# A recurrent attention and a routed mixture of experts on one core: rows gathered by a table of slots, two experts begun during the routing, experts in order of count

## The chip, the cores and the metric

The kernel runs on one core of a Trainium2 chip. The metric is the device time of one execution in microseconds (us). The execution whose profile is shown below took 533.19 us; three other runs took 536.93, 541.19 and 535.67 us.

## The reference

Four sequences of 768 tokens with 8 heads of 48 go through a recurrence with a gate for each channel. Its output, 3072 rows of 384, is the input of a mixture of 16 experts (4 groups of 4). Each token goes to one expert: the best group, and in it the best expert.

```python
f = 1.0 / (1.0 + np.exp(-f_logit))
for t in range(S):                                   # S = 768
    state = f[:, :, t, :, None] * state + np.einsum('bhd,bhe->bhde', k[:, :, t], v[:, :, t])
    y[:, :, t] = np.einsum('bhd,bhde->bhe', q[:, :, t], state)
x = y.transpose(0, 2, 1, 3).reshape(B * S, H * D)    # 3072 x 384
g_idx = np.argmax(x @ w_group, axis=1)               # 4 groups
e_idx = np.argmax(xg @ w_expert[g], axis=1)          # 4 experts in the group
h = np.maximum(xg[mask_e] @ w1[g, e], 0.0)           # 384 -> 1024
out[tok_idx] = (g_w * e_w)[:, None] * (h @ w2[g, e]) # 1024 -> 384
```

Everything is float32. With the inputs of the case the 16 experts get 166 to 243 tokens each.

## The kernel before, in words

**Attention.** The 768 steps are cut into 6 chunks of 128, and each chunk into two units of two sequences, so 12 units. A unit goes through six stages, each written as a Python generator: `gated` (L285 loads f, k, q, v; L289 to L291 the logarithm of the gate; L297 `cs`, its running sum by a matmul with a triangle; L306 and L308 scale q and k into `qh` and `kh`), `turned` (L319 transposes), `scored` (L339 scores `ap`, masked at L341), `weighed` (L355 and L360 the output `y`, L370 the new state), `done` (L391 transposes back, L398 and L403 the router's logits), `routed` (the function `route`). In iteration i of the loop unit i is in `gated`, unit i-1 in `turned`, and so on. The list `WEAVE` says in which order the stages of one iteration take their steps. From that the framework makes one instruction list for each engine; an engine works through its list in order, and so does the queue SP, which issues nearly all the DMAs.

**Routing.** `route` finds, by two one-hot masks, the expert of each token, and by matmuls with a strict triangle (L163 and L166, `rk`) its place among the tokens of that expert; `run` carries the counts from chunk to chunk. L188 then scatters the rows (384 values, the token's number and its weight) to that place in `xs_dram`, a table in DRAM with room for all tokens at every expert. There are four such indirect DMAs for each chunk, issued by POOL. Because an expert's block may be only partly filled, `clear` (L203 and L204) writes zeros over its first 200 rows beforehand, 32 DMAs issued from SP in iterations 2 to 5.

**Experts.** After the loop `fetch` (L556) reads each expert's first 200 rows from `xs_dram`, and the 16 passes follow each other in a fixed order, then two spare passes of 128 rows (`K2 = 2`) for what is beyond 200. A pass is `turn_in` (L581 transposes the rows), `up` (L592, 24 matmuls of width 200, with Relu), `down` (L604, 24 of them), `turn_out` (L611 transposes back, L613 scales, L614 scatters to the output). The weights of three passes are held at a time. `beyond` (L213 to L249) works out what is beyond 200; a loop after it handles what is beyond the spare passes, and does not run with these inputs.

Of the kernel before, what the change touches and what calls it, by code (L numbers as in the profile page):

```python
# [10 lines left out]
FP32 = mybir.dt.float32  # L11
# [11 lines left out]
def kernel(  # L23
# [26 lines left out]
    W = 200  # L50
    K2 = 2
    NOV = K2 + NT + GE - 1
# [5 lines left out]
    assert D == 48 and S % P == 0 and DM == H * D and DM % P == 0 and N == B * S and G == 4 and EG == 4  # L58
# [4 lines left out]
    wp = ctx.enter_context(tc.tile_pool(name="wp", bufs=2))  # L63


    xs_dram = dp.tile([GE * N + P, RW], FP32, name="xs_dram")
# [13 lines left out]
    strict = const([P, P], FP32, "strict")  # L80
# [5 lines left out]
    make_upper_triangular(nc, strict, val=1.0, diag=False)  # L86
    make_identity(nc, ident)
    nc.vector.tensor_copy(strictb, strict)
# [30 lines left out]
    first = iota([P, 4], [[-1, 4]], "first", base=4)  # L119
    firsts = const([P, B * (G + 1), 4], FP32, "firsts")  # L120
    nc.gpsimd.tensor_copy(firsts, first.unsqueeze(1).broadcast_to((P, B * (G + 1), 4)))
    base = iota([P, GE], [[N, GE]], "base")
    lane = iota([P, 1], [[0, 1]], "lane", mult=1)
# [5 lines left out]
    run = const([P, GE], FP32, "run")  # L129

# [3 lines left out]
    def route(c, bs, lgs, rows, sb):  # L134


        nb = len(bs)
        lg, rows = lgs[:, bs[0]:bs[0] + nb, :], rows[:, bs[0]:bs[0] + nb, :]

        def tmp(shape, name, dtype=FP32):  # L140
            return sb.tile(shape, dtype, tag=f"{name}{nb}", bufs=1, name=name)

        SHP = (P, nb * (G + 1), 4)
        L = lg.rearrange("p n (a e) -> p (n a) e", e=4)
        mx = tmp([P, nb * (G + 1)], "mx")
# [4 lines left out]
        nc.vector.scalar_tensor_tensor(out=oh, in0=dl, scalar=0.0, in1=firsts[:, 0:nb * (G + 1), :], op0=OP.is_ge, op1=OP.mult)  # L150
        nc.scalar.activation(dl, dl, AF.Exp)
        yield
        best = tmp([P, nb * (G + 1)], "best")
        nc.vector.reduce_max(out=best, in_=oh, axis=AX)
        nc.vector.tensor_tensor(oh, oh, best.unsqueeze(2).broadcast_to(SHP), OP.is_equal)
        ohv = oh.rearrange("p (n a) e -> p n a e", n=nb)
        ohe = tmp([P, nb, GE], "ohe", BF16)
        nc.vector.tensor_tensor(ohe.rearrange("p n (g e) -> p n g e", e=EG), ohv[:, :, 1:G + 1, :],
                                ohv[:, :, 0, :].unsqueeze(3).broadcast_to((P, nb, G, EG)), OP.mult)
        yield  # L160

        rk = bank([P, nb + 1, GE], "rk")
        nc.tensor.matmul(rk[:, 0:nb, :].rearrange("p n e -> p (n e)"), lhsT=strictb, rhs=ohe.rearrange("p n e -> p (n e)"), start=True, stop=False, skip_group_check=True)  # L163
        for n in range(nb):
            for m in range(n + 1, nb + 1):
                nc.tensor.matmul(rk[:, m, :], lhsT=onesb, rhs=ohe[:, n, :], start=False, stop=(n == nb - 1), skip_group_check=True)  # L166
        pick = tmp([P, nb, GE], "pick")
        nc.vector.tensor_tensor(pick, rk[:, 0:nb, :], run.unsqueeze(1).broadcast_to((P, nb, GE)), OP.add)
        nc.vector.tensor_tensor(pick, pick, ohe, OP.mult)
        place = tmp([P, nb], "place")  # L170
        nc.vector.reduce_sum(out=place, in_=pick, axis=AX)
        placei = sb.tile([P, nb], U32, tag=f"placei{nb}", bufs=2, name="placei")
        nc.vector.tensor_copy(placei, place)
        nc.vector.tensor_tensor(run, run, rk[:, nb, :], OP.add)
        yield
        sm = tmp([P, nb, G + 1], "sm")
# [3 lines left out]
        ew = tmp([P, nb, G], "ew")  # L180
        nc.vector.tensor_tensor(ew, sm[:, :, 1:G + 1], ohv[:, :, 0, :], OP.mult)
        ws = tmp([P, nb], "ws")
        nc.vector.reduce_sum(out=ws, in_=ew, axis=AX)
        nc.vector.tensor_tensor(rows[:, :, DM + 1], ws, sm[:, :, 0], OP.mult)
        nc.gpsimd.tensor_copy(rows[:, :, DM].bitcast(I32), token[:, c, bs[0]:bs[0] + nb])
        yield
        for b in range(nb):
            nc.gpsimd.indirect_dma_start(out=xs_dram[:, :], out_offset=bass.IndirectOffsetOnAxis(ap=placei[:, b:b + 1], axis=0), in_=rows[:, b, :], in_offset=None, bounds_check=GE * N - 1, oob_is_err=False)  # L188
# [3 lines left out]
    gone = const([P, GE, 2], I32, "gone")  # L192
    gone2 = const([P, NOV], I32, "gone2")
    b_expert = const([1, NOV], I32, "b_expert")
    void = const([P, NOV], U32, "void")
    b_row = const([1, NOV], I32, "b_row")
    zero = const([P, RW], FP32, "zero")
    nc.gpsimd.memset(zero, 0.0)
    b_end = const([1, 1], I32, "b_end")


    def clear(e):
        nc.sync.dma_start(out=xs_dram[e * N:e * N + P, :], in_=zero)  # L203
        nc.sync.dma_start(out=xs_dram[e * N + P:e * N + W, :], in_=zero[0:W - P])  # L204

    def beyond(w, skip, sb):
# [4 lines left out]
        SHP = (P, NOV, GE)  # L211
        total = tmp([P, GE], "total")
        nc.vector.scalar_tensor_tensor(out=total, in0=run, scalar=float(w), in1=base, op0=OP.subtract, op1=OP.subtract)  # L213
# [5 lines left out]
        nc.vector.tensor_tensor_scan(end, unit, nb, float(skip), OP.mult, OP.add)  # L219
# [8 lines left out]
        mine = tmp(list(SHP), "mine")  # L228
# [3 lines left out]
        nc.vector.scalar_tensor_tensor(out=off, in0=beg, scalar=-float(P), in1=base, op0=OP.mult, op1=OP.add)  # L232
        nc.vector.tensor_tensor(passed, mine, off.unsqueeze(1).broadcast_to(SHP), OP.mult)
        row = tmp([P, NOV], "row")
        nc.vector.reduce_sum(out=row, in_=passed, axis=AX)
        own = tmp([P, NOV], "own")
        nc.vector.reduce_sum(out=own, in_=mine, axis=AX)
        nc.vector.scalar_tensor_tensor(out=be, in0=blocks, scalar=float(P), in1=own, op0=OP.mult, op1=OP.mult)
        nc.vector.tensor_tensor(row, row, be, OP.add)
        nc.vector.scalar_tensor_tensor(out=row, in0=own, scalar=float(w), in1=row, op0=OP.mult, op1=OP.add)  # L240
        nc.vector.tensor_tensor(mine, mine, run.unsqueeze(1).broadcast_to(SHP), OP.mult)
        nc.vector.reduce_sum(out=own, in_=mine, axis=AX)
        nc.vector.tensor_copy(b_row, row[0:1])
        nc.vector.tensor_scalar(row, row, lane, None, OP.add)
        nc.vector.tensor_tensor(own, row, own, OP.is_ge)
        nc.vector.tensor_scalar(gone2, own, float(SKIP), None, OP.mult)
        nc.vector.tensor_scalar(own, own, -float(SKIP), float(SKIP), OP.mult, OP.add)
        nc.vector.tensor_tensor(void, own, row, OP.add)
        nc.vector.tensor_scalar(b_end, end[0:1, GE - 1:GE], float(K2), None, OP.max)  # L249


    with ExitStack() as fast:
# [7 lines left out]
        for nm, count, fill in (("v", 5, 0.0), ("eq", 2, 1.0), ("qh", 2, 0.0), ("kh", 4, 0.0)):  # L260
            pads[nm] = [kept([P, 2, H, DP], f"{nm}{i}") for i in range(count)]
            for t in pads[nm]:
                nc.gpsimd.memset(t[:, :, :, D:DP], fill)
# [7 lines left out]
        live = {}  # L271

        def heads(t):
            return t.rearrange("p b h d -> p (b h) d")

        def gated(i):

            c, s = units[i]
            w = live[i] = {}
            for nm, src in (("f", f_logit), ("k", k), ("q", q), ("v", v)):  # L280
                if nm == "v":
                    w[nm] = pads["v"][i % 5]
                else:
                    w[nm] = sb.tile([P, 2, H, D], FP32, tag="ld_" + nm, name="ld_" + nm)
                nc.sync.dma_start(out=heads(w[nm])[:, :, 0:D], in_=src[2 * s:2 * s + 2, :, c * P:(c + 1) * P, :].rearrange("b h t d -> t (b h) d"))  # L285

            ex = sb.tile([P, 2, DM], FP32, tag="ex", name="ex")
            nl = ex
            nc.vector.tensor_scalar(ex, w["f"].rearrange("p b h d -> p b (h d)"), -44.0, None, OP.max)  # L289
            nc.scalar.activation(ex, ex, AF.Exp, bias=0.0, scale=-1.0)  # L290
            nc.scalar.activation(nl, ex, AF.Ln, bias=1.0, scale=1.0)  # L291
            eq, qh, kh = pads["eq"][i % 2], pads["qh"][i % 2], pads["kh"][i % 4]
            w.update(eq=eq, qh=qh, kh=kh)
            yield
            for b in range(2):
                cs = bank([P, H, D], "cs")
                nc.tensor.matmul(cs.rearrange("t h d -> t (h d)"), lhsT=tri, rhs=nl[:, b], start=True, stop=True)  # L297
                nc.scalar.activation(eq[:, b, :, 0:D], cs, AF.Exp, bias=0.0, scale=-1.0)
                nc.scalar.activation(kh[:, b, :, 0:D], cs, AF.Exp, bias=0.0, scale=1.0)
                if b:  # L300

                    if s == 0:
                        ends[c] = sb.tile([B, H * DP], FP32, tag="ends", name="ends")
                    nc.scalar.dma_start(out=ends[c][2 * s:2 * s + 2, :], in_=eq[P - 1:P].rearrange("o b h d -> o b (h d)"))
                yield
            nc.vector.tensor_tensor(heads(qh)[:, :, 0:D], heads(w["q"]), heads(eq)[:, :, 0:D], OP.mult)  # L306
# [24 lines left out]
        def scored(i):  # L331
            w = live[i]
            w["am"] = sb.tile([P, 2, 2, HP, P], FP32, tag="am", name="am")
            for b in range(2):
# [73 lines left out]
        def routed(i):  # L408
# [4 lines left out]
            elif s:  # L413
                yield from route(c, tuple(range(B)), *groups[c], sb)
# [285 lines left out]
```

## Time and profile before

| | us |
|---|---|
| profiled execution | 533.19 |
| its span, first to last instruction | 531.4 |
| PE busy | 460.8 |
| first matmul of the attention (L297) | 9.48 |
| last matmul of the routing (L166) | 189.98 |
| first matmul of the experts (L592) | 213.81 |
| last matmul (L611) | 519.7 |
| bytes moved by DMA | 96.35 MB |

PE is TensorE, DVE VectorE, ACT ScalarE, POOL GpSimd. A matmul in float32 is two records in the trace, so 24 matmuls are "x48". "PEclk" is the clock that TensorE was granted, as a share of full speed.

### The profile page before, as it was taken

The page shows a single profiled execution, that of the slowest core. Times are in us where ns is not written, and L with a number is a line of the kernel's source. Part 1 is how long each engine was busy: PE and PEld are TensorE (multiplying, and loading weights), DVE is VectorE, ACT ScalarE, POOL GpSimd, SP SyncE. Part 2 cuts the span into 40 slices and gives each one's busy share as a digit, 9 for nine tenths or more (in the row PEclk, how much of TensorE's full clock was granted, in tenths as well). Part 3 has the DMA queues.
Part 4 walks back from the last instruction along what each step waited for, and adds up shares of the span by engine and source line. Part 5 has one row for each costly group of instructions (what it writes and reads, how often), then busy time and mean ns, then how long its engine had stood idle before and what let it go on. Part 6 is the DMA issues. An engine that isn't in the chain of part 4 may idle for free.

```text
span 531.4 us, 9514 instructions
## 1 busy us (share of the span) xinstructions
PE 460.8 (87%) x3980; PEld 428.6 (81%) x3980; DVE 175.9 (33%) x457; ACT 114.9 (22%) x242; POOL 68.7 (13%) x104
## 2 busy tenths in 40 slices
PE   2668799999999710899999999999999999999991
PEld 0446587777888610899999999999999999999990
DVE  3434157665757422711122212220222022202120
ACT  3545455645542200011001100111001100110000
POOL 5000001211121232000110111010101012011120
PEclk9978799999999955799999999999999999999996
DMA  9599999989971113754757575757575653576200
GB/s 182 63 220 202 222 214 216 199 166 199 302 273 46 46 61 107 270 205 151 260 185 245 166 259 185 262 160 258 178 262 170 240 193 135 161 253 222 78 27 10
DMA packets 140259, 96.35 MB, mean 181 GB/s; under 512 B 105830, under 2 KB 130938, under 8 KB 140208
## 3 DMA queue, kind: packets, MB, share of 16 engines
q1 hardware_dynamic: 136576, 85.85, 59.1%
q0 software_dynamic: 3584, 9.76, 5.2%
q8 instruction: 33, 0.54, 0.4%
q14 instruction: 18, 0.15, 0.1%
q10 hardware_dynamic: 48, 0.05, 0.0%
HBM read 80.89 MB, written 15.39 MB: 181 GB/s over the span
## 4 chain that ended last, share of the span: by engine, by line
PE 71%; issue 6%; DVE 6%; DMA 5%; ACT 3%; POOL 2%; SPq 0%; POOLq 0%; DVEq 0%; ACTq 0%
PE hp L592 27%; PE yo L604 27%; DMA xs_dram<-rows,placei 4%; PE cs L297 3%; PE y_ps L611 2%; PE ap L339 2%; PE y L360 2%; POOL xs_dram L188 2%; PE tr_k L319 2%; DMA ld_f<-in_f_logit_dram 2%; PE xg_ps L581 1%; PE lT L398 1%; PE tr_q L319 1%; PE ds L370 1%; PE x_ps L391 1%
## 5 line engine op out<-in xcount | busy, mean ns | idle before, releaser
L592 PE MATMUL hp<-xe,w 128*128 128x200 f32 (+1 forms) x864 | 146.2, 330 | 1.6 <-DVE xe L582 1.6
L592 PEld LDWEIGHTS hp<-xe,w 128*128 128x128 f32 x864 | 143.4, 193 | 2.1 <-DVE xe L582 2.0
L604 PE MATMUL yo<-h,w 128*128 128x200 f32 (+1 forms) x864 | 144.4, 327 | 0.0
L604 PEld LDWEIGHTS yo<-h,w 128*128 128x128 f32 x864 | 140.3, 190 | 0.0
L614 POOL DMA_INDIRECT out_dram<-yt,to_all x34 | 33.0, 971 | 279.7 <-DVE yt L613 196.5
L594 DVE TENSOR_SCALAR h<-hp 128x400 f32<-128x400 f32 (+1 forms) x36 | 20.1, 558 | 146.9 <-PE hp L592 132.1
L605 ACT COPY yT<-yo 128x200 f32<-128x200 f32 (+1 forms) x36 | 11.5, 319 | 179.0 <-PE yo L604 179.0
L188 POOL DMA_INDIRECT xs_dram<-rows,placei x24 | 25.4, 1057 | 163.0 <-DMA v<-in_v_dram 79.8
L297 PE MATMUL cs<-ex,tri 128*128 128x384 f32 x48 | 25.4, 622 | 22.8 <-ACT ex L291 22.8
L596 ACT ACTIVATE h<-hp 128x400 f32<-128x400 f32 (+1 forms) x36 | 17.6, 490 | 121.7 <-PE hp L592 92.9
L581 PE MATMUL xg_ps<-ident,xg 128*128 128x128 f32 (+1 forms) x102 | 12.4, 258 | 21.7 <-DMA xg<-xs_dram 21.7
L341 DVE TENSOR_TENSOR am<-ap,tri 128x512 f32<-128x512 f32 x48 | 30.6, 681 | 0.6 <-PE ap L339 0.6
L605 DVE COPY yT<-yo 128x200 f32<-128x200 f32 (+1 forms) x18 | 6.4, 358 | 68.5 <-issue 42.2
L581 PEld LDWEIGHTS xg_ps<-ident,xg 128*128 128x128 f32 (+1 forms) x102 | 11.5, 146 | 21.8 <-issue 21.7
L297 PEld LDWEIGHTS cs<-ex,tri 128*128 128x128 f32 x48 | 8.9, 229 | 24.7 <-ACT ex L291 14.4
L339 PE MATMUL ap<-Tq,Tk 48*128 48x128 f32 x384 | 28.1, 286 | 0.0
L339 PEld LDWEIGHTS ap<-Tq,Tk 48*128 48x128 f32 x384 | 23.5, 188 | 3.9 <-issue 3.1
L360 PE MATMUL y<-am,v 128*64 128x128 f32 x384 | 23.6, 276 | 0.0
L360 PEld LDWEIGHTS y<-am,v 128*64 128x64 f32 x384 | 20.7, 137 | 2.0 <-issue 2.0
L319 PE MATMUL tr_q<-ident,qh 128*128 128x128 f32 x96 | 16.3, 295 | 6.3 <-DVE qh L306 5.9
L613 DVE TENSOR_SCALAR yt<-y_ps,xg 128x384 f32<-128x384 f32 (+1 forms) x34 | 19.3, 607 | 4.2 <-PE y_ps L611 4.2
L319 PEld LDWEIGHTS tr_q<-ident,qh 128*128 128x128 f32 x96 | 10.9, 147 | 10.9 <-issue 5.2
(130 smaller groups left out, 386.4 us busy)
## 6 DMA issues: line engine op xcount, KB each, us to landing
w<-in_moe_w_dram SPq DMA_DIRECT2D x36, 1536.0 KB
ld_f<-in_f_logit_dram SPq DMA_DIRECT2D x12, 384.0 KB
ld_k<-in_k_dram SPq DMA_DIRECT2D x12, 384.0 KB
ld_q<-in_q_dram SPq DMA_DIRECT2D x12, 384.0 KB
v<-in_v_dram SPq DMA_DIRECT2D x12, 384.0 KB
xg<-xs_dram SPq DMA_DIRECT2D x18, 193.0 KB
xs_dram<-zero SPq DMA_DIRECT2D x16, 193.0 KB
xs_dram<-zero SPq DMA_DIRECT2D x16, 108.6 KB
```

Source lines behind the costliest of these rows:

```text
L188: nc.gpsimd.indirect_dma_start(out=xs_dram[:, :], out_offset=bass.IndirectOffsetOnAxis(ap=placei[:, b:b + 1], axis=0), in_=rows[:, b, :], ...
L297: nc.tensor.matmul(cs.rearrange("t h d -> t (h d)"), lhsT=tri, rhs=nl[:, b], start=True, stop=True)
L319: nc.tensor.transpose(out=pt[:, a, :], in_=w[nm + "h"][:, b, 2 * a:2 * a + 2, :].rearrange("t r d -> t (r d)"), identity=ident)
L339: nc.tensor.matmul(ap[r][:, a, :], lhsT=w["Tk"][rows, b, a, :], rhs=w["Tq"][rows, b, a, :], start=True, stop=True)
L341: nc.vector.tensor_tensor(w["am"][:, b, r], ap[r], tri.unsqueeze(1).broadcast_to((P, HP, P)), OP.mult)
L360: nc.tensor.matmul(ys[r][DP * b:DP * b + DP, a, :], lhsT=w["v"][:, b, 2 * a + r, :], rhs=w["am"][:, b, r, a, :], start=(c == 0 and a == 0) ...
L581: nc.tensor.transpose(out=pt[:, ko, 0:n], in_=w["x"][0:n, j, ko * P:(ko + 1) * P], identity=ident[0:n, 0:n])
L592: nc.tensor.matmul(hp[:, o, :], lhsT=w1[:, ko, (f + o) * P:(f + o + 1) * P], rhs=w["xT"][:, ko, :], start=(ko == 0), stop=(ko == KO - 1))
L594: nc.vector.tensor_scalar(h[:, f:f + 2, :], hp, 0.0, None, OP.max)
L604: nc.tensor.matmul(yp, lhsT=w2[:, fo, m * P:(m + 1) * P], rhs=w["h"][:, fo, :], start=(fo == 0), stop=(fo == FO - 1))
L613: nc.vector.tensor_scalar(y[0:n], pt[0:n], w["x"][0:n, j, DM + 1:DM + 2], None, OP.mult)
L614: nc.gpsimd.indirect_dma_start(out=out, out_offset=bass.IndirectOffsetOnAxis(ap=w["to"][0:n, j:j + 1].bitcast(U32), axis=0), in_=y[0:n], i ...
```

## The change

The table of places is turned round: instead of scattering each token's row to a place, the kernel writes the rows in the order of the tokens to `x_dram` (two plain DMAs from SP for a unit's rows and a chunk's numbers and weights), and builds in SBUF a `table` that says for every place (16 experts, 256 places) which row belongs there. For each chunk POOL makes, for each of 4 blocks of 128 tokens, a one-hot matrix over 128 lanes (`ln`) and the row's number in two parts at the right expert (`val`); one matmul for each block (`tb`) adds them up. Empty places stay 0 and point to a blank row, so that `clear` and the 32 DMAs of zeros fall away. The rows are then gathered by an indirect DMA (`fetch`).

```diff
-    W = 200
-    K2 = 2
+    WIDE = 2 * P
+    EARLY = 2
+    CLOSE = NC - 3
+    WIDTHS = (230, 222, 214, 212, 208, 204, 200, 196, 193, 191, 189, 186, 182, 174)
...
     def route(...):
+        if tabled:
+            nc.vector.tensor_copy(at[:, :, 0], keys[:, c])
+            nc.vector.tensor_scalar(at[:, :, 1], at[:, :, 0], 7, None, OP.logical_shift_right)
+            nc.vector.tensor_scalar(at[:, :, 0], at[:, :, 0], P - 1, None, OP.bitwise_and)
+            nc.vector.tensor_copy(atf, at)
...
+        nc.sync.dma_start(out=rows_of(c)[:, :, DM:RW], in_=meta)
-        for b in range(nb):
-            nc.gpsimd.indirect_dma_start(out=xs_dram[:, :], out_offset=...placei[:, b:b + 1]..., in_=rows[:, b, :], ...)
+        if tabled:
+            for b in range(B):
+                nc.gpsimd.tensor_scalar(ln, lanes, atf[:, b, 0:1], None, OP.is_equal)
+                for m in range(2):
+                    nc.gpsimd.tensor_scalar(val[:, m], heads_of, atf[:, b, 1:2], part[:, c, b, m:m + 1], OP.is_equal, OP.mult)
+            yield
+            for b, (ln, val) in enumerate(pairs):
+                nc.tensor.matmul(tb, lhsT=ln, rhs=val, start=(b == 0), stop=(b == B - 1))
+            nc.vector.tensor_tensor(table, table, tb, OP.add)
```

Two experts are begun early. After chunk 3 of 0 to 5 (`CLOSE`) `choose_early` ranks the experts by their counts so far; the two fullest have at least 128 tokens by then. Their weights are loaded through a register that SP reads from the table `who`, 128 rows of each are gathered, and a pass of width 128 for each is woven into the last two iterations (`LATE`, where "e" is one step of `early`). At width 128 `down` takes the hidden layer as the stationary operand, 8 matmuls of width 384, and needs no transposes after it.

```diff
+                if c == CLOSE:
+                    choose_early(sb)
+                    for p in range(EARLY):
+                        weights[p] = load_weights(wp, who[0:1, p:p + 1])
+                    first.append(early())
+                    next(first[0])
-        WEAVE = "s t d r s t d r g w w t r w g d t g r d t r g".split()
+        WEAVE = "w d w s d t w d g s d t g r t r g r t r g r t r r".split()
+        LATE = "w d w d d r e r d r e r e r r e r r e r e r".split()
...
+        if n == P:
+            for fo in range(FO):
+                nc.tensor.matmul(yp, lhsT=w["h"][:, fo, :], rhs=w2[:, fo, :], start=(fo == 0), stop=(fo == FO - 1))
+            put(w, 0, P, yp)
+            return
```

After the routing `choose` orders all experts: the two early ones first, with a second pass of width 128 on the same weights, then the other 14 by falling count, each with its width from `WIDTHS` (2801 columns together). The two spare passes fall away. A loop for what is beyond these widths stays, and is passed over when nothing is.

```diff
+    with tc.tile_pool(name="cb", bufs=1) as cb:
+        choose(cb)
-    for p in range(NP):                     # 16 passes of 200, 2 of 128
+    for n in range(GE):                     # 2 passes of 128, 14 of WIDTHS
```

In the attention the loads of unit i+1 are issued ahead of iteration i, q is loaded straight into `qh` and the gate is worked out in the place where f was loaded, one of the two copies of L392 goes to ACT, the small DMA of `ends` is issued by SP instead of ACT, and the routing follows one iteration earlier, in one call for a whole chunk (before, the last chunk was routed in two halves).

```diff
+            load(i + 1)
-            nc.scalar.dma_start(out=ends[c]..., in_=eq[P - 1:P]...)
+            nc.sync.dma_start(out=ends[c]..., in_=eq[P - 1:P]...)
-                nc.vector.tensor_copy(x[:, :, :, r, :], pt...)
+                (nc.scalar.copy if r else nc.vector.tensor_copy)(x[:, :, :, r, :], pt...)
-            if 2 <= i < 6:
-                for e in range(GE // 4):
-                    clear((i - 2) * GE // 4 + e)
```

## The prediction

> **What bounds the kernel now.** I read the page's busy shares and slices first, then the windows, then the timelines and the chain of waits inside each stage.
>
> ```profile
> PE 460.8 (87%) x3980; PEld 428.6 (81%) x3980; DVE 175.9 (33%) x457; ACT 114.9 (22%) x242; POOL 68.7 (13%) x104
> PE   2668799999999710899999999999999999999991
> PEclk9978799999999955799999999999999999999996
> ```
>
> TensorE sets the time nearly everywhere, except in slices 1 to 5 and in slices 14 to 16, where its clock is cut as well. The windows put numbers to that (columns: window, length, busy time of PE, weight loads, DVE, ACT and POOL, clock, DMA share, GB/s):
>
> ```profile
> 0.00:60.00 60.00, 34.84 (x314) 25.13 (x314) 22.96 (x38) 27.16 (x47) 7.46 (x39) 0.90 1.00 171
> 60.00:156.00 96.00, 92.10 (x1292) 75.12 (x1291) 56.78 (x135) 50.38 (x102) 12.80 (x13) 0.97 1.00 231
> 190.00:214.00 24.00, 1.63 (x11) 1.35 (x12) 6.29 (x28) 0.00 (x0) 5.71 (x6) 0.50 0.30 101
> 214.00:520.00 306.00, 304.69 (x1927) 303.47 (x1927) 67.43 (x173) 29.11 (x72) 34.02 (x35) 0.99 0.57 195
> ```
>
> From 60 to 156 and from 214 to 520 nothing but less or faster TensorE work helps. From 0 to 60 PE is idle for 25 us. From 190 to 214 it does nothing: the chain there is the scatters, each waiting for the one before.
>
> ```profile
> 199.13 2.59 DMA xs_dram<-rows,placei
> 202.52 0.98 POOL xs_dram L188
> 205.39 2.65 DMA xs_dram<-rows,placei
> ```
>
> In the first 60 us the timeline of SP shows why: f of unit 2 (25.04) and of unit 3 (37.57) are issued late, behind the router's small loads and then behind the zeros.
>
> ```profile
> 18.81 6.13 SPq L104 DMA_DIRECT2D gw<-in_moe_w_expert_dram  x4
> 25.04 0.42 SPq L285 DMA_DIRECT2D ld_f<-in_f_logit_dram  x1
> 34.69 0.89 SPq L203 DMA_DIRECT2D xs_dram<-zero  x1
> 37.57 0.39 SPq L285 DMA_DIRECT2D ld_f<-in_f_logit_dram  x1
> ```
>
> **Start: -9.7 us.** `cs` of units 2 to 5 starts at 31.35, 44.19, 58.91 and 74.16. The four last small loads took 6.13 us, 4.5 of them on the `ends` DMA of unit 1; in the changed list of SP that DMA stands behind the loads of unit 2. Units 0 and 1 bring 3.1 MB, 17 us at the 182 GB/s of the first slice, and one round of small DMAs more, so f of unit 2 is issued at about 21 and `cs` comes 4 us earlier (27.3). Without the zeros (30.5 to 37.5) f of unit 3 is issued by 28 and TensorE becomes the limit: some 8 us of its list lie between the two, so `cs` at 38.5 instead of 44.2. Units 4 and 5 follow at 51.5 and 64.5 (11.7 and 13 us of work), 9.7 us early; then 13 us an iteration as before (74.2 to 152.9 in six). Bounds: -4 if only unit 2 gains, -15 if all the lost time of units 2 to 5 comes back. The loads' new release (f after `cs`, q through `qh`) costs nothing while the prefetch is a unit ahead; without it, up to 4 us a unit.
>
> **The table on TensorE's path: +30 us.** This is the step I weigh most. In the changed kernel's list for PE, each chunk's `rk` is followed by only four transposes (0.66 us) and then by the four `tb` matmuls, each waiting for POOL; all of the next iteration stands behind them. What must happen in between: on DVE pick, pick, run, keys (165.43 to 166.16 for the like, 0.75), `qh` and `kh`, which stand between them in DVE's list (0.96 each, 1.8 together), three more small ones (0.5): 3.1 us. Then POOL's 12. Before has no such operation; its nearest rows are
>
> ```profile
> masks.py:66 POOL TENSOR_SCALAR_AFFINE_SELECT tri<-tri 128x128 f32<-128x128 f32 x1 | 0.3, 282 | 0.0
> L185 POOL COPY rows<-token 128x2 int32<-128x2 int32 x2 | 0.3, 187 | 1.7 <-DMA xs_dram<-rows,placei 1.7
> ```
>
> so 0.28 for `ln` and 0.2 for each `val`, 0.68 a block and 2.7 a chunk. Together 5.8, less 0.7 for transposes and the few `y` matmuls: a wait of 5.1 us. Then the clock:
>
> ```profile
> 31.35 1.65 PE L297 MATMUL cs<-ex,tri 128*128 128x384 f32 x2 [5.63 <-ACT ex L291]
> 74.16 0.91 PE L297 MATMUL cs<-ex,tri 128*128 128x384 f32 x2
> ```
>
> after 5.6 idle us the same matmul takes 1.65 instead of 0.91, and so on for 3.5 us, 1.5 us lost. Chunks 0 to 3: 4 x 6.6 = 26.4. Chunk 4 has no `qh` and `kh` in between: 5.9. Off that go 2.3 of the 3.9 us that PE waits from 60 to 156 anyway. Bounds: 16 (pitch of POOL's smallest rows, 0.13, and no clock loss) and 46 (0.5 us for each POOL operation); I take the value of the nearest shapes.
>
> The Trainium skill, page "GPSIMD Engine Reference", sections "Elementwise — side-by-side cycle accounting" and "Engine selection", speaks against this placing: ordinary elementwise work belongs on VectorE, which is about twice as fast for two inputs. DVE's rows (0.23 for 128x80, 0.16 for 128x16) doubled would make a block 1.3 us instead of 0.68, 2.4 more a chunk, and the sum over six chunks 14 us worse (about 539).
>
> **Beside other work, at nothing.** One copy a unit more on ACT (0.55, ACT is busy 50 of 96 us), `at` on DVE (57 of 96), the `ends` DMA on SP (needed an iteration later by the transposes of the gate; late, it would hold PE 2 us a chunk), the rows' DMAs (as many bytes as the scatters). `choose_early`, some 17 DVE operations of 0.2, lies beside `tb` and `y`. SP then waits for `who`; behind it stand the last rows' DMAs, wanted only by the last gathers. The early weights, 6.3 MB, take 23 us at the 270 GB/s seen from 140 to 160, and are wanted some 28 us later; if late, PE waits for the difference.
>
> **End of routing: +3 and -1.4 us.** Before, the last `y` ends at 180.3 and the last `rk` at 190.2: 9.9 us, half of it waits. Now the transposes of the early rows (0.7) and six of their eight `up` groups (8 x 1.34 = 10.7 together, from a 5.36 pass) fill this, so 12.9: +3. Then 23.6 us to the first `hp` (213.81) before. Now: 2 on DVE without `qh`, 2.8 on POOL, 5 in all beside the last `up` groups (2.7); from the last `tb` the two early `down`, 8 x 0.65 each (10.4), lie beside `choose`, 16 DVE operations, eight of them 256 wide (0.43): 5.5; the next eight entries of POOL's list, gathers and one scatter, 7 us at 0.97; the first main gather lands 2.6 to 3 later, transposes and copy 1.2: 17.2. Sum 22.2: -1.4. Bounds: -5 if POOL's entries overlap, +14 if each has to wait out the last as the scatters do (2.9 apart).
>
> **Expert passes: -37.1 us.** One pass of 200 in the chain:
>
> ```profile
> 243.05 8.12 PE hp L592 x48
> 251.17 0.65 PE y_ps L611 x6
> 251.83 0.52 PE xg_ps L581 x6
> 252.35 8.17 PE yo L604 x48
> 487.39 5.36 PE hp L592 x48
> ```
>
> From 128 and 200 wide: 24 matmuls take 24 x (0.019 + 0.0016 w). Fourteen widths, 2801 columns: 48 x (14 x 0.019 + 0.0016 x 2801) = 228; transposes 14 x 1.18 = 16.5; two passes of 128: 2 x (5.36 + 5.2 + 0.33) = 21.8. Sum 266, with 3 for a ramp at half clock and one gap 269, against 305.9 (213.81 to 519.7). Bounds -34 and -39. It rests on weights: 3.1 MB plus rows in 15.4 to 19 us, up to 243 GB/s, where slices reached 302. The reference's inputs give the 14 experts 166 to 199 tokens, each 4 or more below its width, and the early two 169 and 142 at chunk 3 and 243 and 222 in all, so no block is left over.
>
> **Tail: +3.** The last pass now has two blocks, so two scatters, the second after the first.
>
> Sum: -9.7 + 30 + 3 - 1.4 - 37.1 + 3 = -12.2, so the span goes from 531.4 to 519.2 and the profiled execution from 533.19 to 521.0. That one lies 3.7 under the runs' median (536.93), to which 524.7 answers. A change of about 1% is what a measurement of this kernel can tell.
>
> **Rivals.**
> 1. Slower: POOL's one-hot operations are dear. There are 72 of them, on PE's path in all six chunks, taken at 0.23 on average. From 0.40 the gain is gone; at 0.5 it is +19.5: 544. For: DVE's first operation took 3.27 us instead of 0.55 beside POOL's memsets, so the two slow each other. Against: POOL's own rows there kept their length (0.30 for 128x256). Chance 0.2.
> 2. The `tb` waits are covered, because PE arrives later than I think: no +30, 494.7. For: the `rk` before hang on a DVE chain too and waited 0.4 us at most inside the loop. Against: four transposes are all that lies between. Chance 0.18.
> 3. POOL's indirect DMAs go one by one, 2.9 apart: +15, 539.7. For: every one of the scatters did. Against: those wrote one table, the gathers write different tiles. Chance 0.1.
> 4. That the change does not do what it says (blocks left over for the loop) is excluded by the counts.
>
> The forecast has 0.52. The range takes in rival 2 nearly and rival 1: 498 to 546; the forecast's own, from its bounds, 510 to 538. Faster by over 1%: rival 2 and most of the forecast, 0.64; slower by over 1%: most of rival 1 and a little of rival 3, 0.2; within 1%, 0.16.
>
> **What would show it.** Right: `cs` of unit 5 near 65; five idle gaps of 4 to 6 us ahead of `tb` in the attention, released by POOL, with slow matmuls after; first main `hp` about 20 us later than before (near 234), the last matmul near 503. Wrong: no idle time ahead of `tb`, a first `hp` near 205 (rival 2), POOL operations over 0.4 us (rival 1), a main stage that waits for weights or lasts over 272 us.

## The result, and the profile after

The changed kernel takes 564.51 us (median of four runs, 564.0 to 566.92) against 536.77 for the kernel before: a ratio of 1.0509, 95% interval 1.0443 to 1.0575. It is slower by 5%, where 524.7 and "faster" had been forecast. The profiled execution took 564.0 us, its span is 561.8 where the sum had 519.2. The page's busy line, its PE slices and its clock slices:

```profile
PE 470.8 (84%) x3855; PEld 422.7 (75%) x3855; DVE 169.5 (30%) x435; ACT 115.8 (21%) x245; POOL 114.4 (20%) x197
PE   2689689597795958781999999979999979999990
PEclk9789979689696877977899999999999998999996
```

TensorE has fewer matmuls than before (3855 against 3980) and is busy longer (470.8 against 460.8), and the columns are fewer too (2801 and four passes of 128 against 16 passes of 200 and two of 128), so many ran at a low clock: slices 6 to 20 have both holes and clocks down to 0.6, where before had a full stretch from slice 6 to 13. The windows by stage (window, length, busy time of PE, weight loads, DVE, ACT and POOL, clock, DMA share, GB/s):

```profile
0.00:60.00 60.00, 42.52 (x456) 32.92 (x456) 27.61 (x48) 32.38 (x61) 8.10 (x57) 0.91 0.93 182
60.00:156.00 96.00, 75.99 (x961) 62.01 (x957) 43.87 (x122) 38.54 (x78) 18.23 (x39) 0.82 0.52 111
233.00:266.70 33.70, 17.53 (x74) 10.88 (x74) 15.45 (x52) 0.38 (x1) 19.16 (x24) 0.79 0.51 157
266.70:548.20 281.50, 272.93 (x1644) 264.13 (x1644) 50.23 (x110) 24.79 (x60) 52.46 (x49) 0.99 0.50 172
```

The start gained what it should (42.52 us of work in the first 60, 34.84 before). The second row is the heart of it: 75.99 of 96 us busy at 0.82, against 92.10 at 0.97. The third is the way from the last routing to the first main pass, 33.8 us, half of it idle. The fourth is the main stage: 281.5 us, with 8.6 idle. One table in TensorE's timeline (start, length, and in brackets the idle time ahead and what ended it):

```profile
64.78 0.40 PE L194 MATMUL rk<-ohe,onesb 128*128 128x16 bf16 x10
65.03 0.63 PE L501 MATMUL tr_k<-ident,kh 128*128 128x128 f32 x4
70.32 0.21 PE L233 MATMUL tb<-val,ln 128*128 128x64 bf16 x1 [4.66 <-POOL val L228]
70.47 0.69 PE L539 MATMUL y<-Tq,st 48*64 48x128 f32 x2
71.80 0.21 PE L233 MATMUL tb<-val,ln 128*128 128x64 bf16 x1 [0.65 <-POOL val L228]
...
74.91 1.97 PE L539 MATMUL y<-Tq,st 48*64 48x128 f32 x26
76.80 1.94 PE L574 MATMUL lT<-xT,gw 128*64 128x128 f32 x16
```

One wait of 4.66 us, three of 0.65, and then 26 records of `y` in 1.97 us and `lT` in 1.94, where all 32 of `y` take 1.10 and `lT` 1.09 at full clock (the rows of e6 below). The iteration of the loop that holds this lasts 22.93 us (`cs` from 63.02 to 85.95), the next one without a table 11.94. The groups name the cause:

```profile
L225 POOL TENSOR_SCALAR ln<-lanes,atf 128x128 bf16<-128x128 f32 x24 | 14.4, 599 | 191.9 <-DVE atf L207 191.9
L228 POOL TENSOR_SCALAR val<-heads_of,atf,part 128x32 bf16<-128x32 f32 x48 | 22.1, 471 | 0.0
L233 PE MATMUL tb<-val,ln 128*128 128x64 bf16 x24 | 5.1, 211 | 36.3 <-POOL val L228 36.3
```

A one-hot operation takes 0.60 or 0.47 us on GpSimd, 0.51 on average, not 0.23; TensorE idles 36.3 us for them in all. At the end of the routing it waits once more, for rows:

```profile
232.99 0.40 PE L194 MATMUL rk<-ohe,onesb 128*128 128x16 bf16 x10
241.32 12.79 PE L397 MATMUL yo<-w,h 128*128 128x384 f32 x32
265.23 0.87 PE L368 MATMUL xg_ps<-ident,xg 128*128 128x128 f32 x3 [11.11 <-DMA xg<-x_dram,rows_p]
```

In the span, step by step (us; the prediction's times are against the span of 531.4):

| | before | predicted | after | off by |
|---|---|---|---|---|
| `cs` of unit 5 | 74.16 | 64.5 | 63.02 | -1.5 |
| last `rk` | 189.98 | 213.3 | 232.96 | +19.7 |
| last `rk` to first main `hp` | 23.8 | 22.2 | 33.8 | +11.6 |
| first main `hp` to last matmul | 305.9 | 269 | 281.5 | +12.5 |
| last matmul to end | 11.7 | 14.7 | 13.6 | -1.1 |

The last four rows add up, but for rounding, to the 42.6 us between 519.2 and 561.8. So three places were to be explained.

### The profile page after: what moved, and what is told of

It is laid out like the page before. It is cut to its first block, busy times and chain, and to the rows that moved or that the text cites. A ratio compares the mean times of both kernels' runs of the same rounds, so it can differ in the third digit from the quotient of the medians.

```text
span 561.8 us, 9341 instructions
## 1 busy us (share of the span) xinstructions
PE 470.8 (84%) x3855; PEld 422.7 (75%) x3855; DVE 169.5 (30%) x435; ACT 115.8 (21%) x245; POOL 114.4 (20%) x197
## 5 line engine op out<-in xcount | busy, mean ns | idle before, releaser
L378 PE MATMUL hp<-xe,w 128*128 128x128 f32 (+14 forms) x864 | 140.1, 323 | 1.6 <-DVE xe L369 1.6
L404 PE MATMUL yo<-h,w 128*128 128x230 f32 (+13 forms) x672 | 118.5, 337 | 0.0
L404 PEld LDWEIGHTS yo<-h,w 128*128 128x128 f32 x672 | 114.7, 192 | 0.5
L389 POOL DMA_INDIRECT out_dram<-yt,xg x32 | 34.7, 1083 | 196.0 <-DVE yt L388 142.8
L380 DVE TENSOR_SCALAR h<-hp 128x256 f32<-128x256 f32 (+14 forms) x36 | 19.5, 541 | 146.9 <-PE hp L378 146.9
L382 ACT ACTIVATE h<-hp 128x256 f32<-128x256 f32 (+14 forms) x36 | 17.2, 478 | 140.7 <-PE hp L378 140.7
L355 POOL DMA_INDIRECT xg<-x_dram,rows_p x30 | 33.2, 1106 | 49.3 <-issue 36.0
L479 PE MATMUL cs<-ld_f,tri 128*128 128x384 f32 x48 | 23.0, 570 | 15.6 <-ACT ld_f L473 15.6
L233 PE MATMUL tb<-val,ln 128*128 128x64 bf16 x24 | 5.1, 211 | 36.3 <-POOL val L228 36.3
L539 PEld LDWEIGHTS y<-Tq,st 48*64 48x64 f32 x320 | 16.4, 174 | 16.2 <-issue 16.1
L368 PEld LDWEIGHTS xg_ps<-ident,xg 128*128 128x128 f32 (+14 forms) x96 | 10.4, 143 | 22.0 <-issue 11.9
L539 PE MATMUL y<-Tq,st 48*64 48x128 f32 x320 | 25.6, 352 | 0.0
```

What stands on the lines that cost most here:

```text
L355: nc.gpsimd.indirect_dma_start(out=w["x"][0:m, j, :], out_offset=None, in_=x_dram[0:1 + top, :], in_offset=bass.IndirectOffsetOnAxis(ap=ro ...
L368: nc.tensor.transpose(out=pt[:, ko, 0:m], in_=w["x"][0:m, j, ko * P:(ko + 1) * P], identity=ident[0:m, 0:m])
L378: nc.tensor.matmul(hp[:, o, :], lhsT=w1[:, ko, (f + o) * P:(f + o + 1) * P], rhs=w["xT"][:, ko, :], start=(ko == 0), stop=(ko == KO - 1))
L380: nc.vector.tensor_scalar(h[:, f:f + 2, :], hp, 0.0, None, OP.max)
L382: nc.scalar.activation(h[:, f:f + 2, :], hp, AF.Relu)
L389: nc.gpsimd.indirect_dma_start(out=out, out_offset=bass.IndirectOffsetOnAxis(ap=w["x"][0:m, j, DM + 1:RW].bitcast(U32), axis=0), in_=y[0:m ...
```

## The experiments

Each timed run had the kernel before on the same chip; its medians were 534.5 to 539.1 us.

**e1: the one-hot operations on VectorE.**

```diff
-                nc.gpsimd.tensor_scalar(ln, lanes, ...)
+                nc.vector.tensor_scalar(ln, lanes, ...)
-                    nc.gpsimd.tensor_scalar(val[:, m], heads_of, ...)
+                    nc.vector.tensor_scalar(val[:, m], heads_of, ...)
```

> The changed kernel with its 72 one-hot operations (ln, val) on VectorE instead of GpSimd, at the same places of the program. In the changed kernel (564.5 us) the 12 operations of a chunk take 6.2 us on GpSimd (0.60 for ln, 0.46 for val) and TensorE idles 4.4 to 5.1 us ahead of the first tb and 0.65 ahead of each of the other three. Theory (the one-hot operations are what tb waits for): at the 0.18 to 0.24 us of VectorE's rows for 128x32 and 128x80 the twelve take about 2.5 us, so 3.7 us less a chunk in six chunks, and up to 1 us less of slow clock in each: 22 to 28 us gained, 537 to 543 us, the last rk 18 to 23 us earlier than 232.96. Rival (VectorE's own chain ahead of the one-hot operations and the slow clock after a gap set the wait): VectorE has 2.5 us more to do in each chunk, so 558 us or more.

Measured: 539.28 us, ratio 1.0109 (1.0043 to 1.0176). The groups of the same three lines:

```profile
L225 DVE TENSOR_SCALAR ln<-lanes,atf 128x128 bf16<-128x128 f32 x24 | 6.8, 284 | 0.2
L228 DVE TENSOR_SCALAR val<-heads_of,atf,part 128x32 bf16<-128x32 f32 x48 | 12.1, 299 | 0.0
L233 PE MATMUL tb<-val,ln 128*128 128x64 bf16 x24 | 5.4, 227 | 17.7 <-DVE val L228 17.7
```

They overlap, so that a block comes every 0.61 us instead of 1.48; the wait halves, and the last `rk` is at 213.69, 0.4 from the prediction's 213.3: with a block about as cheap as it had taken (0.68), its sum for the routing holds. Its parts hold less well. From `cs` of unit 5 to the last `rk` this run takes 150.1 us and e2 (below, with the table off TensorE's path) 116.2, so the table on TensorE's path costs 33.9 us there, where 30 were forecast, and the rest is 2.6 shorter than forecast. Of the 33.9 only 17.7 are waits, where the five forecast waits make 24.8; the other 16.2, the low clock among them, were not divided further. The theory stands; where the operations run is worth 25 us.

**e2: the table's matmuls one iteration later.** The one-hot operations stay on GpSimd, the `tb` matmuls and the add move into the next iteration's first routing step (with the choice of the early experts); chunk 5's stay.

```diff
-            tb = bank([P, 2, GE, 2], "tb")
-            ...
+            def settle():    # the four tb and the add
+                ...
+            if c < NC - 1:
+                owed.append(settle)
+            else:
+                settle()
...
+            elif owed:
+                owed.pop()()
+                if c == CLOSE + 1:    # choose_early and what follows
```

> The changed kernel with the four tb matmuls of a chunk (and the table's add, and after chunk 3 the choice of the early experts) put off by one iteration of the attention loop, chunk 5's excepted; the one-hot operations stay on GpSimd. Theory (the cost is the placing: TensorE reaches tb before GpSimd is done, idles and then runs at a low clock): an iteration with a table takes 23 to 24 us in the changed kernel and one without 11.94, so four of 11 to 12.2 and about 9.5 in chunk 4 come back, less 2 for what the first gap hides: 50 to 56 us, so 508 to 515 us, with no idle time over 1 us ahead of tb in chunks 0 to 4. Rival (the one-hot operations' time has to be waited out somewhere, since GpSimd or VectorE have no room): 535 us or more, with new idle time ahead of cs, ap or rk.

Measured: 513.51 us, ratio 0.9627 (0.9548 to 0.9706), already faster than the kernel before. The window that had 75.99 busy at 0.82:

```profile
60.00:156.00 96.00, 95.72 (x1474) 81.38 (x1470) 65.78 (x190) 53.30 (x113) 27.91 (x54) 1.00 0.67 166
```

Nothing idles, POOL does even more in it, and an iteration with a table lasts 11.91 us (62.83 to 74.74). So the price of an operation matters only because nothing lies between `rk` and `tb`; the placing costs 51 us.

**e3 and e6: TensorE's wait filled with matmuls that nobody reads.** In e3 30 ahead of the first `tb` and 4 ahead of each other one, in e6 42 and 12 (ahead of the first one fewer in chunks 4 and 5; in e3 8 ahead of each other one of chunk 5). The edit of e6:

```diff
             for b, (ln, val) in enumerate(pairs):
+                for _ in range(12 if b else (42, 30, 4)[max(0, c - 3)]):
+                    nc.tensor.transpose(out=idle, in_=tri, identity=ident)
                 nc.tensor.matmul(tb, lhsT=ln, rhs=val, ...)
```

> The changed kernel with transposes of a constant that nobody reads put into TensorE's wait: 30 ahead of the first tb of chunks 0 to 3, 22 in chunk 4 and 2 in chunk 5, and 4 (8 in chunk 5) ahead of each later tb, at 0.15 us each about as long as the idle time they replace. Theory (about 4.5 us of each chunk's cost is not the wait but the low clock after it, which an idle TensorE brings): y, lT and the next y run at 1.1, 1.1 and 1.9 us again and 4 us a chunk come back in five chunks: 542 to 548 us. Rival (they are slow for a reason of their own, not because of the idle time): they stay at 1.97 and up to 3.4 us, and the time is 564 us or more by what the filling overruns.

> As the filled gap before, in which the filling transposes took 0.115 us each, not 0.15, so that TensorE still idled 1.40 and three times 0.83 us a chunk, and the clock fell all the same. Now 42 of them ahead of the first tb (30 in chunk 4, 4 in chunk 5) and 12 ahead of each later one, as long as the whole wait or a little longer. Theory (any idle time of TensorE, even with 60% of the wait filled, brings the low clock): y and lT run at 1.1 us and the next y at 1.9, 3 us a chunk come back in five chunks, less what the filling overruns: 550 to 558 us. Rival (the low clock comes from something else in that place): y, lT and the next y take 2.0, 2.0 and 2 to 3.4 us as before, 564 us or more.

Measured: e3 565.67 us (ratio 1.0595, 1.0524 to 1.0665), e6 559.0 (1.0377, 1.0303 to 1.0451). e3, the last filling and what follows, then e6 in the same place:

```profile
74.47 0.21 PE L236 MATMUL tb<-val,ln 128*128 128x64 bf16 x1 [0.83 <-POOL val L228]
74.61 1.98 PE L542 MATMUL y<-Tq,st 48*64 48x128 f32 x32
76.53 1.97 PE L577 MATMUL lT<-xT,gw 128*64 128x128 f32 x16
```

```profile
74.33 0.19 PE L236 MATMUL tb<-val,ln 128*128 128x64 bf16 x1
74.44 1.10 PE L542 MATMUL y<-Tq,st 48*64 48x128 f32 x32
75.48 1.09 PE L577 MATMUL lT<-xT,gw 128*64 128x128 f32 x16
```

With 5.33 of the 9.3 us (65.17 to 74.47) filled (e3) the clock falls all the same, filled whole it does not: it is TensorE's idle time that brings the low clock. Not any idle time does, as e6's theory had it: in its chunk 1 waits of 1.26 and 0.34 us are left, TensorE is busy for 10.41 of the 12 us from 97 to 109, and the clock is 1.00 there and in the 6 us behind. The expectation of e3, 542 to 548, was wrong, because the filling ran at 0.115 us each and left holes. In e6 the last `rk` is 9.8 us earlier (223.15), 0.5 of it already at the first `rk`; the other 9.3 are what the low clock costs the routing, some 1.9 us a chunk. Half of it is lost again in the main stage, whose waits for rows are then longer (one of 5.58 us), and the time came out 1 us above the range expected.

**e4: buffers of their own for the rows of the first two main passes.**

```diff
-        return n, fetch(ep, rows_p[:, n, 1:2], P)
+        return n, fetch(ep, rows_p[:, n, 1:2], P, xp=mo)    # xg from the pool mo, a tag of its own
```

> The changed kernel with the gathered rows of the first two main passes in buffers of their own, so that their gathers need not wait until the scatters of the early passes have read the old ones. In the changed kernel TensorE idles 11.1 us ahead of the first main transposes (265.23). Theory (the two gathers stand behind the scatter of the first early expert and seven other entries of GpSimd's list): the first one is issued at about 247.6 and lands by 254.5, so the first main hp comes 9 to 10 us earlier and the time is 554 to 557 us. Rival (the gathers themselves are slow to land, some 17 us after issue, or what follows is late by as much): 562 us or more.

Measured: 552.64 us, ratio 1.0365 (1.0297 to 1.0434). In the changed kernel's POOL timeline the gather that TensorE waits for is the eighth entry (258.96), and that of the second pass comes after both early scatters (266.59):

```profile
247.59 1.04 POOL L355 DMA_INDIRECT xg<-x_dram,rows_p  x1 [6.42 <-issue]
250.34 1.04 POOL L389 DMA_INDIRECT out_dram<-yt,xg  x1 [0.30 <-DVE more L315]
258.96 0.96 POOL L355 DMA_INDIRECT xg<-x_dram,rows_p  x1 [0.31 <-issue]
262.72 1.03 POOL L389 DMA_INDIRECT out_dram<-yt,xg  x1 [0.30 <-issue]
266.59 0.99 POOL L355 DMA_INDIRECT xg<-x_dram,rows_p  x1 [2.84 <-DMA out_dram<-yt,xg]
```

With buffers of their own the two gathers are first (246.33 and 247.68), the wait is 1.25 us and the first main `hp` is at 254.94, 11.8 us earlier. The theory stands; the gain is 1.4 us above its range.

**e5: six buffers instead of four for the rows of the other passes.**

```diff
-        ... tag="xg", bufs=2 if pool is ep else 4, ...
+        ... tag="xg", bufs=2 if pool is ep else 6, ...
```

> The changed kernel with six buffers instead of four for the gathered rows of the passes, so that a gather need not wait until the scatters three passes back have read theirs. In the changed kernel TensorE waits 7.7 us in six places for gathered rows from 280 us on (the longest 3.3), the gathers being issued some 3 to 4 us after the two weight loads of 1.5 MB each. Theory (they land late because they are issued behind the weights): issued a pass earlier they are there in time, no idle time ahead of the transposes after 290, and with the low clock after the two longest waits 8 to 10 us come back: 554 to 557 us. Rival (the DMA engines are simply too busy, and weights then come late by as much): 561 us or more, with idle time ahead of hp or yo instead.

Measured: 554.39 us, ratio 1.0314 (1.0262 to 1.0366): 10 us, and no wait of TensorE from 290 us on; the main stage takes 270.5 us instead of 281.5. What it took away, in the changed kernel (POOL, SP and PE timelines):

```profile
352.82 1.52 POOL L389 DMA_INDIRECT out_dram<-yt,xg  x1 [2.58 <-DMA out_dram<-yt,xg]
361.33 1.00 POOL L355 DMA_INDIRECT xg<-x_dram,rows_p  x1 [6.98 <-issue]
```

```profile
357.74 0.37 SPq L347 DMA_DIRECT2D w<-in_moe_w_dram  x1
358.61 0.51 SPq L345 DMA_DIRECT2D w<-in_moe_w_dram  x1
```

```profile
370.24 0.42 PE L368 MATMUL xg_ps<-ident,xg 76*128 76x76 f32 x3 [1.59 <-DMA xg<-x_dram,rows_p]
463.17 0.40 PE L368 MATMUL xg_ps<-ident,xg 61*128 61x61 f32 x3 [3.25 <-DMA xg<-x_dram,rows_p]
```

The profile names no releaser for the gather. That it waited for the scatter above it, which frees its buffer and landed 7.4 us after issue, is read from the times: all ten such gathers from 338 us on are issued 0.8 to 1.1 us after the landing of the scatter ahead of them. It is then issued after 3 MB of weights instead of before them, its two blocks land 6.7 and 7.6 us later, and that is just too late (waits of 1.30 and 1.59 us). The theory stands for these. The longest wait, 3.25 us at 463.17, has another cause, which the theory did not name: the gather of its 61 rows.

```profile
449.37 1.02 POOL L355 DMA_INDIRECT xg<-x_dram,rows_p  x1 [2.33 <-PE yo L404]
450.70 1.69 POOL L355 DMA_INDIRECT xg<-x_dram,rows_p  x1 [0.31 <-issue]
```

The scatter ahead had landed after 2.5 us, and the next weights were issued only at 451.20 and 452.07. The 128 rows of 449.37 landed after 3.2 us, the 61 rows of 450.70 after 12.4. With six buffers the 61 rows took 13.1 us, but were issued two passes earlier.

**e7: the early experts' passes only behind the last routing.** The "e" steps leave the list `LATE`.

> The changed kernel with the two fullest experts still chosen after chunk 3 and loaded, but their passes begun only behind the last routing (transposes, up and down all after it). Prediction's reading (the up groups fill TensorE's waits in the last routing and cost 3 us there): taking them out lets the last rk come some 10 us earlier, at 222 to 224, but 11.4 us of up groups then follow it; as TensorE idles 11.1 us there anyway, waiting for the first main rows, these cover the wait: 558 to 564 us. Rival (the early start is worth its work, 11 us or more, because the wait behind the routing cannot be covered, the main gathers standing behind the early scatters): 570 us or more.

Measured: 562.92 us, ratio 1.0456 (1.0401 to 1.0511). The last `rk` comes at 224.50 (8.5 us earlier), the first main `hp` at 263.66 (3.1 earlier). The start ahead of time is worth nothing here: its up groups delay the last `rk`, and run behind it they cover a wait that is there anyway.

**e10: equal widths.** `WIDTHS = (200,) * 14`, 2800 columns instead of 2801.

> The changed kernel with fourteen passes of 200 columns instead of 230 falling to 174 (2800 columns instead of 2801; the experts taken in the same order, each still fitting). Theory (a pass costs TensorE 24 matmuls of a fixed part and a part that goes with the columns, so only the sum of the columns counts): 562 to 567 us, the same within what can be measured. Rival (the falling widths themselves are worth something, since the long passes come first and cover the early gathers): 570 us or more.

Measured: 549.72 us, ratio 1.0245 (1.0208 to 1.0282). Both theories were wrong: equal widths are 14.8 us faster. The matmuls are the same (fourteen `hp` of 8.28 us are 115.9, the falling ones add up to 116.0), but TensorE no longer waits for rows from 280 us on; the first main `hp` is 3.0 us earlier, the main stage 11.3 shorter. The scatters of a pass's second block, 72 rows, landed 2.4 to 2.6 us after issue, wherever the trace tells it; with falling widths some took 6 to 8.

**e13 and e14: which widths.** e13 has fourteen widths of 222, second blocks of 94 rows. e14 has falling widths again, of the same sum 2801, but second blocks of 96, 96, 84, 84, 80, 78, 72, 70, 65, 64, 60, 56, 56 and 48 rows.

> The changed kernel with fourteen widths of 222, so that every pass has a second block of 94 rows (3108 columns, 23.6 us more matmul work than with 200 by the prediction's formula); one look, for the scatters' times from issue to landing. With falling widths the second blocks' scatters landed after 3.8, 7.4, 6.3, 2.6, 2.5, 3.7, 2.5, 3.6, 2.5, 2.8, 8.0 and 5.4 us in order of time, with blocks of 72 rows always after 2.4 to 2.6. Theory (the number of rows decides): blocks of 94 rows land after 7 us or more in nearly every pass, and TensorE waits for gathered rows in most of them. Rival (the pass or the experts' own row counts decide): the times differ from pass to pass as with falling widths, some of them under 3 us.

> The changed kernel with other falling widths of the same sum, 2801 columns, whose second blocks (96, 96, 84, 84, 80, 78, 72, 70, 65, 64, 60, 56, 56 and 48 rows) all have a divisor between 12 and 16. Theory (a scatter or gather is spread over as many DMA engines as the largest divisor of its rows, up to 16; 94, 86, 61 and 58 rows have 2, 2, 1 and 2, take 5 to 8 us to land and push the next gathers behind the weight loads): all scatters of the main stage land in 2.4 to 4 us, no wait for gathered rows from 290 us on, 549 to 553 us as with equal widths. Rival (the falling as such costs it, the long passes first and the short ones last): 560 us or more.

Measured: e13 612.48 us in a single execution; its second blocks' scatters landed after 6.0 to 7.4 us in all thirteen passes for which the trace tells it (7 or more had been expected), and TensorE waited nine times for rows, 21.1 us in all. e14 551.44 us, ratio 1.0217 (1.0176 to 1.0259), the scatters from 329 us on 2.4 to 3.8 us, one wait of 0.2 us. So it is neither the falling nor the pass: it is the row count, and the section on the hardware says which.

**e11: the val operations issued twice.**

> The changed kernel with each of the 48 val operations on GpSimd issued twice (the same values written again). Theory (the one-hot operations lie on TensorE's path one for one): 8 more of 0.46 us in each of six chunks, 3.7 us a chunk, 22 us in all: 584 to 590 us, the block's pitch ahead of tb 2.4 us instead of 1.48. Rival (part of GpSimd's work is covered, or the wait is set by VectorE's chain ahead of it): 576 us or less.

Measured: 582.68 us, ratio 1.0853 (1.0803 to 1.0902), 1.3 us under the range. TensorE's wait ahead of `tb` grows from 36.3 to 58.0 us, which is the 48 operations of 0.46, and the span by 19.1: nearly one for one.

**e8, e9 and e12: the repairs together.** e8: `tb` put off (e2), chunk 5's one-hot operations alone on VectorE, the buffers of e4 and of e5. e9: chunk 4's on VectorE as well, and all but one of the early up groups behind the last `rk`. e12: e9 with equal widths.

> The changed kernel with four repairs: tb put off by one iteration (chunk 5's excepted), the one-hot operations of chunk 5 alone on VectorE, buffers of their own for the rows of the first two main passes, six buffers for the rows of the others. Theory (each of the four costs was shown or is about to be, and they lie in different stages): from 513.5 us with tb put off alone, 12 for the buffers of the first two passes, 3.5 for chunk 5's operations, 8 for the rows of the main passes: 488 to 492 us, first main hp near 198, main stage 273 us long. Rival (they cover one another, the wait only moves): the first main hp after 206 and 500 us or more.

> The repaired kernel (486.9 us) with two more edits: the one-hot operations of chunk 4 on VectorE as well, and only one of the early experts' eight up groups ahead of the last rk instead of six, the others behind it. In the repaired kernel TensorE waits 2.6 us for chunk 4's table and then runs its 60 up matmuls in 8.21 us instead of 6.9, and idles 4.47 us ahead of the first main transposes, whose passes then run at a low clock (7.66 us instead of 5.62). Theory (the up groups only delay the last rk, and behind it they cover the wait for the first gathered rows): the last rk comes 8 to 9 us earlier than 180.0, the first main hp 4 to 5 us earlier than 199.98, at full clock: 479 to 483 us. Rival (the chain from the last rk through the table, the choice and the gathers sets the end, and becomes longer by what VectorE has more to do): 486 us or more.

> The kernel of e9 (478.4 us) with fourteen equal widths of 200 instead of falling ones. Theory (the falling widths cost time only through gathers issued behind the weights, which six buffers cure): 477 to 480 us, the same within what can be measured, since the sum of the columns is the same. Rival (they cost something by themselves, in the early passes, the late ones or the end): 474 us or less.

Measured: e8 486.89 us, ratio 0.9051 (0.9005 to 0.9098); e9 478.4, ratio 0.8930 (0.8886 to 0.8975). The costs add: 51.0 (e2), 11.9 (e4) and 10.1 (e5) taken from 564.5 leave 491.5; the last 4.6 us go with chunk 5's operations, expected at 3.5, which were not run by themselves. The two times lie 1.1 and 0.6 us under their ranges. e9's page, and its way from the last `rk` to the first main `hp`:

```profile
PE   1679999999999789899999999999999999999980
PEclk9789999999999989999999999999999999999996
```

```profile
170.19 0.19 PE L191 MATMUL rk<-ohe,strictb 128*128 128x64 bf16 x1 [1.69 <-DVE ohe L186]
181.80 10.49 PE L404 MATMUL yo<-w,h 128*128 128x384 f32 x32
193.46 5.62 PE L385 MATMUL hp<-xe,w 128*128 128x128 f32 x48 [0.85 <-DVE xe L376]
```

e12 took 487.02 us, ratio 0.9134 (0.9053 to 0.9215), which neither theory had. From the second main pass to the last matmul it takes as long as e9 (262.4 us from 208.77, 262.8 from 200.13), as the first theory says; ahead of that, one copy out of `hp` is some 8 us late (197.78 in e9):

```profile
206.31 0.39 ACT L389 ACTIVATE h<-hp 128x256 f32<-128x256 f32 x1 [10.35 <-remote]
```

The profile names no instruction of this core as what ended that wait ("remote"). Its cause was not found and stays open.

## Why the prediction was wrong, point by point

**Start: right in sum, partly by luck.** `cs` of units 2 to 5 at 29.98, 40.52, 51.08 and 63.02, forecast 27.3, 38.5, 51.5 and 64.5. Units 2 and 3 came 2.7 and 2.0 us late, and units 4 and 5 made up for it: they took 10.6 and 11.9 us, where the times of the forecast have 13 each. (Its own 11.7 and 13 us of work would have made 50.2 and 63.2.)

**The table: right mechanism and place, wrong price.** Idle gaps ahead of `tb`, released by POOL, slow matmuls after them: all as forecast. The term that failed is "0.28 for `ln` and 0.2 for each `val`": they take 0.60 and 0.47. The nearest rows of before were other forms of operation, and the smaller of them has two columns. So rival 1, at 0.2, was the case, and its sign, POOL operations over 0.4 us, was there. It had priced 0.5 us at +19.5 for six chunks; the last `rk`, which has only five of them ahead of it, is 19.7 later than forecast. Of that, 60 operations at 0.51 instead of 0.23 us make 16.8, and the low clock, sized at 1.5 us a gap and about 1.9 (e6), 2 more; that the two figures agree is partly luck. With cheap operations the last `rk` comes at the forecast time (e1). The reason given for rival 1, that VectorE and POOL slow each other, was not the cause: while POOL worked on the first chunk's twelve operations (68.75 to 74.7), VectorE stood idle:

```profile
75.01 0.22 DVE L234 TENSOR_TENSOR table<-table,tb 128x64 f32<-128x64 f32 x1 [6.37 <-PE tb L233]
```

Against rival 1 I had put that POOL's own rows kept their length beside VectorE's work; that says nothing on a form that POOL had not run.

The Trainium skill's rule that I weighed and set aside, page "GPSIMD Engine Reference", section "Engine selection", has GpSimd about twice as slow as VectorE for elementwise operations with two inputs, and calls one input "roughly line-rate". `ln` and `val` have one input tensor and a scalar for each lane, so the rule does not cover them as it stands; still its factor was nearer than the rows I chose: `ln` took 0.60 us against 0.28 on VectorE (e1), 2.1 times, and `val` 0.47 against 0.30, 1.6 times. (Twice the prediction's rows of 0.23 and 0.16 make 1.1 us a block, not 1.3; a block took 1.48.)

**End of routing: wrong step, the gathers.** Forecast: 7 us for eight entries, 2.6 to 3 to land. Measured: 11.4 (247.59 to 258.96) and 6.1. I priced the entries and not the reason why that gather is the eighth: it needs a buffer that the early scatter has to free. Rival 3 had the entries 2.9 us apart; they are 1.3 to 2.3 apart, and the buffers are the mechanism (e4). Another 3.3 us is chunk 5's one-hot operations (6.1 us, forecast 2.8). The parts of the sum make 16.3 to 16.7 us, not its 17.2.

**Expert passes: columns right, rows missed.** Matmuls by columns are right within some 2% (`hp` of 230 took 9.48 us, formula 9.29). What failed is "Bounds -34 and -39. It rests on weights": it rests on the gathered rows, which no step of mine followed once the first had landed. The stage took 281.5 us, over the 272 that were named as a sign of being wrong, and 270.5 with six row buffers (e5), near the forecast 269; row counts that land quickly do nearly the same (e10, e14).

**Tail and early experts.** The tail came out 1.1 better. The two early passes fill the routing's waits as said, and bring nothing (e7).

The range's upper end, 546, held rival 1 alone. The three faults lie in different stages, and each by itself would have left the time at most at 544; no case had two of them together.

## What to carry to other kernels

When a change gives an engine an operation that the trace does not show, price it on the engine's own scale from both sides, and ask first whether anything lies between producer and consumer: with other work between them the price did not matter (e2), without it 22.1 us more of such operations made the span 19.1 longer (e11). For a gather into reused buffers, follow what frees the buffer and what is issued meanwhile; buffers to spare made the widths harmless (e9). Choose row counts of indirect DMAs that have a large divisor up to 16, for gathers too.

## What the runs showed of the hardware

**Indirect DMAs by row count.** Time from issue to landing of a scatter of n rows of 1536 bytes, in the main stage of the changed kernel (128 where no weights were under way):

| rows | largest divisor up to 16 | rows for each | us |
|---|---|---|---|
| 128, 84, 80, 72, 65, 54 | 16, 14, 16, 12, 13, 9 | 8, 6, 5, 6, 5, 6 | 2.5 to 2.6 |
| 63 | 9 | 7 | 2.8 |
| 102, 68, 76 | 6, 4, 4 | 17, 17, 19 | 3.6 to 3.8 |
| 46 | 2 | 23 | 4.0 |
| 58 | 2 | 29 | 5.4 |
| 86 | 2 | 43 | 6.3 |
| 94 | 2 | 47 | 7.4 |
| 61 | 1 | 61 | 8.0 |

While the 94 rows were under way and hardly anything else, the DMA share (next to last column) was about the 0.125 of two engines in 16:

```profile
356.00:357.00 1.00, 1.00 (x8) 1.00 (x6) 0.00 (x0) 0.00 (x0) 0.00 (x0) 1.00 0.14 32
357.00:358.00 1.00, 1.00 (x7) 1.00 (x7) 0.00 (x0) 0.26 (x1) 0.00 (x0) 1.00 0.14 33
```

e13 (94 rows in every pass, 6.0 to 7.4 us) and e14 (divisors from 12 up, second blocks in 2.4 to 3.1 us where the trace tells it) were chosen by this and bear it out. The Trainium skill states it, page "DMA: Bandwidth & Descriptors", section "Why a DMA increments its semaphore by 16 and not by 1": a DMA is spread over the largest number of engines up to 16 that divides the slowest dimension (of size above 1) on both of its sides. The table agrees; the engines themselves are not counted in the traces. The prediction did not draw on this.

**GpSimd's small operations.** 128x128 takes 0.60 us and 128x32 0.47, on VectorE 0.28 and 0.30: `ln`, with four times the columns of `val`, does one operation and `val` two, so these runs do not part the cost of a column from that of an operation.

**The clock.** A wait of 9.3 us filled to 57% lowers TensorE's clock as an empty one does; filled whole, it does not (e3, e6). With TensorE busy for 10.41 of 12 us (e6, chunk 1) the clock stayed at 1.00.
